# Decay attention into a three-way-max MLP: rows of decays on another DMA queue, head transposes in halves, the second batch's softmax sums on TensorE

## The chip, the cores and the metric

One core of a Trainium2 chip. The metric is the device time in microseconds of one execution. Engines: TensorE (PE, its weight loads PEld), VectorE (DVE), ScalarE (ACT), GpSimd (POOL) and SyncE (SP, which only issues DMAs here).

## The reference

Inputs: q, k, v of (8 batches, 8 heads, 576 positions, 64), decays f of (8, 8, 576), three weights of 512x768 and one of 768x512, all fp32 in effect.

```
scores = q k^T / 8 + cum[:, None] - cum[None, :]     # cum = cumsum(log(clip(f)))
scores = where(causal, -1e9, scores);  scores -= max(scores)
attn = exp(scores);  attn /= sum(attn) + 1e-9;  o = attn v
x = o as (4608 tokens, 512)
out = max(x w1, x w2, x w3) w_out                    # (4608, 512)
```

## The kernel before

Heads are numbered n = 0 to 63, eight to a batch; two heads are a pair. A head's scores are held transposed, keys on partitions and queries on columns, in two units: unit 2 has the first 256 queries (blocks of keys 0 and 1: 384 columns of scores), unit 1 the other 320 (1216 columns over five blocks of keys). For each unit: scores on TensorE into PSUM, a maximum over keys (DVE over the blocks, L695 to L706, then a POOL all-reduce over partitions, L716), the maximum subtracted by a further matmul pass, exp on ACT into probabilities (L734), and later the product with v (`values`).

**Batch 0** is treated apart. Its raw heads are loaded by SP (`load_raw`, L456) and transposed on TensorE by matmuls with an identity (`turn_head`, L463): for each of q and k three matmuls of 128 columns, whose result in PSUM holds even and odd positions of the head on the two halves of the partitions. Three of four copies to SBUF are ACT's (L481), one is DVE's (L479); each writes every second element of the head's row. Four PSUM banks serve two heads' turns. The cumulated decays are made in `decay` (L413): a scan on DVE, then row 64 of each head's keys is filled, for heads 0 and 1 by ACT itself and for heads 2 to 7 by six DMAs of 2304 bytes that ACT issues (L439). [...] Its sums of probabilities come from a column of ones beside v.

**Batches 1 to 7** use operands that are split in two fp32r parts; raw q and k are loaded four heads at a time (`load_quad`, L525), transposed and split by DVE and ACT, and rearranged into QS and KS by DMAs (`load_head`, L566). Their sums of probabilities are made outside TensorE (end of `scores`, L740 to L759): DVE adds the blocks of keys (L744 to L750; ACT copies 128 columns at L753), POOL adds over the partitions (L758) into Z, SP copies row 0 of Z into SC (`sums_row`, L862), and `finish_pair` (L867) adds 1e-9, takes the reciprocal, writes it to DRAM and reads it back spread over 64 partitions for each head, and multiplies the pair's output. The values of a pair (`values_pair`, L791) are fp32 matmuls of 64 weight columns each, one head in the lower and one in the upper half of the partitions of one PSUM bank (L802), five or two blocks of keys long.

**The MLP** of batch b (`moe`, L949) has 432 fp32r matmuls of 128x128 weights against 256 or 320 tokens (L906) and then the output matmuls of 512 columns (L935). It runs among the attention of batch b + 1. The weights (24 loads of 512 KB, L508) are split into two fp32r parts by ACT and DVE (L512 to L522) during batch 0.

**The order** is written by a planner (`Plan`, L49): each step is added with an engine, an estimated cost, the keys that it reads and writes and a priority; `emit` simulates the engines, takes from the ready steps of an engine the one with the lowest rank (priority less a share BLW of the work that hangs on it, L99) and so fixes each engine's program order. LAG, MORE and LATE are its delays between engines. A DMA step may not start before the eighth DMA before it is over (L137). [...]

Of the kernel before, what the change touches and what calls it, by code (L numbers as in the profile page):

```python
# [48 lines left out]
class Plan:  # L49
# [9 lines left out]

    ROOM = {"PE": (0.93, 0), "ACT": (1.0, -20.0), "DVE": (1.0, 0.0), "POOL": (1.0, 400.0), "SP": (1.0, 0)}  # L60
    LATE = 350.0
    MORE = (0.0, 100.0, 0.0, 0.0, 250.0)
    LIKE, HOLD = 4.0, 0.4

    def __init__(self):
# [21 lines left out]
    def emit(self):  # L87
# [8 lines left out]
        for i in reversed(range(n)):  # L96
            s = self.steps[i]
            down[i] = s[1] + s[5] + max((down[u] + 150 for u in users[i]), default=0.0)
        BLW = 0.21  # L99
        rank = [s[4] * 1.0 - BLW * down[i] / 12000 for i, s in enumerate(self.steps)]  # L100
        free, wait, live = {}, {}, {}
        for i, s in enumerate(self.steps):
# [8 lines left out]
        while done < n:  # L111
            best = None
            for e in free:
                t = free[e] if live[e] else (max(free[e], wait[e][0][0]) if wait[e] else None)
                if t is not None and (best is None or t < best[0]):
                    best = (t, e)
            t, e = best
            while wait[e] and wait[e][0][0] <= t:
                _, i = heapq.heappop(wait[e])
                heapq.heappush(live[e], (rank[i], i))  # L120

            here = live[e][0]
# [12 lines left out]
            if self.steps[i][5]:  # L135

                t = max(t, lanes[-8])  # L137
            begin[i] = t
            cost = (self.steps[i][1] - saved) * self.ROOM[e][0] + self.ROOM[e][1]
            end = t + cost  # L140
            if e == "PE":
                end = clock.run(t, cost, self.steps[i][6])
            free[e] = end
            done += 1
            if self.steps[i][5]:

                if self.steps[i][5] < 50 and e == "ACT":
                    end += 1850
                else:
                    end = moved = max(moved, end + 650) + self.steps[i][5]  # L150
                end += self.LATE
                lanes.append(end + 650)
            for u in users[i]:
                same = self.steps[u][0] == e
                lag = self.LAG["SP" if self.steps[i][5] else e][self.ENGINES.index(self.steps[u][0])]
                lag = 0 if same and e == "PE" else lag + self.MORE[self.ENGINES.index(self.steps[u][0])]
                ready[u] = max(ready[u], end + lag)
                left[u] -= 1
                if not left[u]:
                    heapq.heappush(wait[self.steps[u][0]], (ready[u], u))  # L160
# [24 lines left out]
def kernel(  # L185
# [18 lines left out]
    P = 128  # L204
# [44 lines left out]


    HEADS = [[sb(t, [P, 2 * S])] for t in ("qs0", "qs1", "ks0", "ks1")]
    for t in ("xh", "xl"):
        buf = sb(t, [P, 2, 2 * S])
        HEADS.append([buf[:, 0], buf[:, 1]])
    KQ = [x for group in HEADS for x in group]
    KF, QF = [x[:, 0:S] for x in KQ], [x[:, S:] for x in KQ]

# [28 lines left out]
    RAW = [sb(f"w{i}", [P, 1024], I32) for i in range(NW)]  # L286


    RAWQK = [x.bitcast(F32)[0:96, 0:768].rearrange("p (c x) -> p c x", c=2) for x in RAW[NW - H:]]
    spare = sb("hdl", [P, 512 + 2 * P], I32)  # L290
    XW = [sb("o", [P, 512], I32), spare[:, 0:512]]

# [120 lines left out]
    def decay():  # L413
# [18 lines left out]
        for n in range(2):  # L432
# [2 lines left out]
        c8 = UT[KT - 1][0:H, :]  # L435
        add("DVE", 540, lambda: nc.vector.tensor_scalar(c8, ft[0:H, :], -1.0 / scale, None, op0=ALU.mult),
            ["pf1"], [f"u{KT - 1}"], DP)
        for n in range(2, H):
            add("ACT", 600, lambda n=n: nc.scalar.dma_start(out=KF[n][64:65, :], in_=c8[n:n + 1, :]),  # L439
                [f"u{KT - 1}"], [f"kf{n}/2"], DP + n, 2304 / 360)  # L440
        add("DVE", 369, lambda: nc.vector.tensor_scalar(cs[:, 0, :], ft, -1.0, None, op0=ALU.mult),
            ["pf1"], ["cs"], DP)
        add("DVE", 669, lambda: nc.vector.scalar_tensor_tensor(
# [12 lines left out]
    def load_raw(n, prio):  # L456
        b, h = n // H, n % H
        for c, src in ((1, k), (0, q)):
            add("SP", 560, lambda c=c, src=src: nc.sync.dma_start(
                out=RAWQK[n][:, c], in_=src[b, h].rearrange("(p x) d -> p (x d)", p=96)),  # L460
                [], [f"raw{n}/{c}"], prio, 147456 / 330)

    def turn_head(n, prio):  # L463


        for c, buf, kc in ((0, QF, "qf"), (1, KF, "kf")):
            ps, kp = ((MPS[0], "mp0"), (MPS[1], "mp1"), (MPS[2], "mp2"), (TPS, "t0"))[2 * (n % 2) + c]

            def go(ps=ps, c=c):
                for a in range(3):  # L470
                    nc.tensor.matmul(ps[:, 96 * a:96 * a + 96], RAWQK[n][:, c, P * a:P * a + P],
                                     IDF[0:96, 0:96], start=a == 0, stop=True, skip_group_check=True)

            add("PE", 3 * 225, go, [f"raw{n}/{c}", "idf"], [kp], prio, rows=96)
            dst = buf[n][0:D, :].rearrange("d (p a e) -> d e a p", a=3, e=2)
            for e in range(2):
                src = ps[D * e:D * e + D, 0:288].rearrange("d (a p) -> d a p", a=3)
                if c == 0 and e == 0:
                    add("DVE", dve_cost(288), lambda dst=dst, src=src: nc.vector.tensor_copy(dst[:, 0], src), [kp], [f"{kc}{n}/0"], prio)  # L479
                else:  # L480
                    add("ACT", act_cost(288) + 115 * e, lambda dst=dst, src=src, e=e: nc.scalar.activation(  # L481
                        dst[:, e], src, AF.Copy), [kp], [f"{kc}{n}/{e}"], prio)


    def load_weights(step, prio):
# [131 lines left out]
    def scores(n, unit, prio):  # L617
# [111 lines left out]
        for bk, w, col in d["exps"]:  # L729
            if first:  # L730
                key = PFKEYS.get((unit, bk), [f"pf{name}"])
            else:
                key = [f"{pk}/{bk}"] if unit == 1 else [pk]
            add("ACT", act_cost(w), lambda bk=bk, w=w, col=col: nc.scalar.activation(  # L734
                px()[:, col:col + w], bank[bk][:, 0:w], AF.Exp, scale=sc), [kb[bk]], key, prio)
        if first:
            return


# [15 lines left out]
            add("DVE", dve_cost(P), add_blocks, [pk], ["s2/1"], prio + SP_)  # L755
        else:
            add("DVE", sum(dve_cost(w) for w in (320, 320, 192, 64)), add_blocks, [pk], ["s1"], prio + SP_)
        add("POOL", 450 + 2.6 * nq, lambda: nc.gpsimd.partition_all_reduce(  # L758
            Z[:, q0:q0 + nq], blocks_sum()[:, q0:q0 + nq], P, bass.bass_isa.ReduceOp.add), [f"s{unit}"], [f"z{unit}"], prio + SP_)  # L759

    def values(n, unit, prio):
# [29 lines left out]
    def values_pair(n, unit, prio):  # L791
# [74 lines left out]

    def finish_pair(pi, prio):  # L867
        i = pi % NU
        add("DVE", 130, lambda: nc.vector.tensor_scalar(SC, SC, 1e-9, None, op0=ALU.add), ["sc"], ["sc"], prio)
        add("DVE", 180, lambda: nc.vector.reciprocal(SC, SC), ["sc"], ["sc"], prio)  # L870
        row_dma(lambda: rdram[pi].rearrange("t (p c) -> (t p) c", p=32), lambda: SC, ["sc"], [f"rd{pi}"], prio)
        for j in range(2):
            row_dma(lambda j=j: R()[64 * j:64 * j + 64, :], lambda j=j: rdram[pi, j:j + 1, :].broadcast_to((64, S)),
                    [f"rd{pi}"], [f"r/{j}"], prio, 150000)
        add("DVE", dve_cost(S), lambda: nc.vector.tensor_tensor(U(i), U(i), R(), op=ALU.mult), [f"u{i}", "r"], [f"u{i}"], prio)

    def split_x(b, prio):
# [100 lines left out]
    QP = -0.2  # L978
    UO = 1
    LO = -2.55  # L980
    UP, VO, FO, XO = 0.4, 1.8, -0.95, -2.7
    HP, VP = -1.8, 0.35
    SP_ = 1.05
    HC, VO1, XO1, QP1, CB = -0.8, -1.0, -0.3, 0.4, -0.15
    order = (1, 2) if UO else (2, 1)
    for n in range(H):
        load_raw(n, n - 9.9)
    for n in range(H):
        turn_head(n, n - 5.1)
        if n % 2 == 0:  # L990
            load_v(n // 2, n - LEAD - VP)
    for unit, up in ((2, 0.0), (1, 0.5)):
# [27 lines left out]
    lag = 0.0  # L1020
# [63 lines left out]
```

## Time and profile before

| | |
|---|---|
| median of 3 runs | 915.48 us (915.07 to 915.65) |
| the profiled execution's own time | 919.88 us |
| its span, first to last instruction | 918.1 us |
| mean granted TensorE clock | 0.996 |
| PE busy | 896.9 us (98%), 6394 matmul records |
| PEld busy | 807.9 us (88%) |
| DVE busy | 678.9 us (74%) |
| ACT busy | 392.7 us (43%) |
| POOL busy | 455.4 us (50%) |
| queue of SP's DMAs | 94802 packets, 109.14 MB |
| queue of ACT's DMAs | 192 packets, 0.01 MB |

How to read it: the profile is of one execution, and the time of that execution lies 4.4 us above the median of the runs. Busy times of engines overlap; the end comes where one engine's work and its waits add up. Records of matmuls overlap one another (they are pipelined and their ends are modelled).

### The profile page before, as it was taken

The page shows a single profiled execution, that of the slowest core. Times are in us where ns is not written, and L with a number is a line of the kernel's source. Part 1 is how long each engine was busy: PE and PEld are TensorE (multiplying, and loading weights), DVE is VectorE, ACT ScalarE, POOL GpSimd, SP SyncE. Part 2 cuts the span into 40 slices and gives each one's busy share as a digit, 9 for nine tenths or more (in the row PEclk, how much of TensorE's full clock was granted, in tenths as well). Part 3 has the DMA queues.
Part 4 walks back from the last instruction along what each step waited for, and adds up shares of the span by engine and source line. Part 5 has one row for each costly group of instructions (what it writes and reads, how often), then busy time and mean ns, then how long its engine had stood idle before and what let it go on. Part 6 is the DMA issues. An engine that isn't in the chain of part 4 may idle for free.

```text
span 918.1 us, 17938 instructions
## 1 busy us (share of the span) xinstructions
PE 896.9 (98%) x6394; PEld 807.9 (88%) x6394; DVE 678.9 (74%) x1491; ACT 392.7 (43%) x900; POOL 455.4 (50%) x395
## 2 busy tenths in 40 slices
PE   6999999999999999999999999999999999999998
PEld 5899987888989898998989898998989898998998
DVE  5899998697958777796967777697877867662211
ACT  5897644444334433443334443344333434332111
POOL 4461456756455556546465464646556564641000
PEclk8999999999999999999999999999999999999999
DMA  7946245555435554634444454544464454401000
GB/s 219 304 130 165 65 125 135 154 119 133 131 98 141 129 144 113 157 91 127 127 117 130 121 156 105 135 118 106 118 143 148 105 152 117 116 14 37 1 35 24
DMA packets 95082, 110.29 MB, mean 120 GB/s; under 512 B 51617, under 2 KB 62625, under 8 KB 94994
## 3 DMA queue, kind: packets, MB, share of 16 engines
q1 hardware_dynamic: 94802, 109.14, 45.1%
q8 instruction: 51, 0.84, 0.4%
q14 instruction: 37, 0.30, 0.1%
q10 hardware_dynamic: 192, 0.01, 0.0%
HBM read 49.56 MB, written 9.86 MB: 65 GB/s over the span
## 4 chain that ended last, share of the span: by engine, by line
PE 74%; DVE 13%; DMA 5%; SPq 3%; issue 2%; ACT 2%; POOL 1%; ACTq 0%; DVEq 0%; POOLq 0%
PE mp L906 40%; PE mp L935 15%; PE s L646 10%; PE t L802 7%; DVE mx L706 2%; DVE va_s L750 2%; DMA w<-in_moe_w_dram 1%; DVE hl L535 1%; DVE tm L915 1%; SPq L368 1%; PE t L771 1%; DMA hl<-in_k_dram 1%; SPq L566 1%; DMA hl<-in_q_dram 1%; POOL z L758 1%
## 5 line engine op out<-in xcount | busy, mean ns | idle before, releaser
L906 PE MATMUL mp<-xh_r,w_r 128*128 128x320 f32 (+1 forms) x2160 | 461.6, 298 | 4.0 <-ACT tm L913 2.2
L906 PEld LDWEIGHTS mp<-xh_r,w_r 128*128 128x128 f32 x2160 | 355.6, 188 | 14.4 <-issue 5.4
L906 PE MATMUL mp<-xl_r,w_r 128*128 128x320 f32 (+1 forms) x1080 | 319.6, 296 | 0.0
L758 POOL PARTITION_ALL_REDUCE z<-va_s x112 | 226.2, 2019 | 183.1 <-DVE va_s L750 78.9
L716 POOL PARTITION_ALL_REDUCE gm<-mx x131 | 158.3, 1209 | 175.4 <-DVE mx L706 95.6
L906 PEld LDWEIGHTS mp<-xl_r,w_r 128*128 128x128 f32 x1080 | 203.3, 188 | 0.6
L915 DVE TENSOR_TENSOR tm<-mp,tm 128x256 f32<-128x256 f32 (+1 forms) x192 | 86.7, 452 | 68.3 <-PE mp L906 62.4
L646 PEld LDWEIGHTS s<-qs_r,ks_r 128*128 128x128 f32 (+1 forms) x784 | 115.1, 181 | 22.6 <-issue 14.5
L646 PE MATMUL s<-qs_r,ks_r 128*128 128x320 f32 (+4 forms) x784 | 131.4, 286 | 1.8 <-POOL qs_r L719 0.7
L935 PE MATMUL mp<-w_r,hmh_r 128*128 128x512 f32 (+1 forms) x396 | 123.3, 393 | 0.8 <-ACT w_r L521 0.6
L706 DVE TENSOR_TENSOR mx<-mx,s 128x320 f32<-128x320 f32 (+3 forms) x248 | 92.2, 372 | 21.5 <-PE s L646 12.1
L918 ACT ACTIVATE hmh_r<-tm 128x256 fp32r<-128x256 f32 x96 | 39.8, 414 | 127.6 <-DVE tm L915 127.1
L935 PEld LDWEIGHTS mp<-w_r,hmh_r 128*128 128x128 f32 x396 | 70.3, 188 | 16.5 <-issue 3.2
L935 PE MATMUL mp<-w_r,hml_r 128*128 128x512 f32 (+1 forms) x198 | 76.9, 388 | 0.0
L535 DVE STREAM_TRANSPOSE hl<-hl 128x576 f32<-128x576 f32 x56 | 68.6, 1243 | 3.7 <-DMA hl<-in_k_dram 3.6
L734 ACT ACTIVATE pf<-s 128x512 f32<-128x512 f32 (+4 forms) x107 | 49.1, 504 | 42.6 <-PE s L646 37.2
L913 ACT ACTIVATE tm<-mp 128x256 f32<-128x256 f32 (+1 forms) x96 | 39.4, 411 | 59.9 <-PE mp L906 55.5
L920 DVE TENSOR_TENSOR hml_r<-tm,hmh_r 128x256 fp32r<-128x256 f32 x96 | 48.9, 510 | 12.8 <-ACT hmh_r L918 12.6
L675 DVE TENSOR_TENSOR s<-s,mask 128x256 f32<-128x256 f32 x96 | 40.4, 421 | 21.3 <-PE s L646 21.2
L719 POOL CAST qs_r<-gm 1x256 fp32r<-1x256 f32 (+1 forms) x112 | 52.0, 464 | 7.2
L734 ACT ACTIVATE ph_f<-s 128x384 f32<-128x384 f32 x80 | 35.9, 505 | 39.9 <-PE s L646 34.8
L935 PEld LDWEIGHTS mp<-w_r,hml_r 128*128 128x128 f32 x198 | 37.2, 188 | 8.3
(207 smaller groups left out, 1281.0 us busy)
## 6 DMA issues: line engine op xcount, KB each, us to landing
qs_r<-hl SPq DMA_DIRECT2D x168, 144.0 KB, 2.6
ks_r<-hl SPq DMA_DIRECT2D x168, 144.0 KB, 2.7
w<-in_moe_w_dram SPq DMA_DIRECT2D x18, 512.0 KB, 6.3
out_dram<-o_r SPq DMA_DIRECT2D x35, 256.0 KB, 2.7
hl<-in_q_dram SPq DMA_DIRECT2D x14, 576.0 KB, 5.1
hl<-in_k_dram SPq DMA_DIRECT2D x14, 576.0 KB
r_r<-rdram SPq DMA_DIRECT2D x56, 144.0 KB, 3.0
vn<-in_v_dram SPq DMA_DIRECT2D x30, 128.0 KB, 5.1
```

The source lines that it names most:

```text
L535: add("DVE", 1085, lambda e=e, tt=tt, xs=xs: nc.vector.transpose(tt[:, e], xs[:, e]), [key + "0"], [key + "1"], prio)
L646: nc.tensor.matmul(bank[bk][0:l.shape[-1], col:col + w], l, rhs(qa, w), start=start and bk not in begun, stop=stop, skip_group_check=True)
L706: nc.vector.tensor_tensor(mt[:, a:a + w], mt[:, a:a + w], bank[bk][:, col:col + w], op=ALU.max)
L716: add("POOL", 450 + 2.6 * nq, lambda: nc.gpsimd.partition_all_reduce(gm, mt, P, bass.bass_isa.ReduceOp.max), [km, km + "a"], [kg], prio - CB)
L719: add("POOL", 130 + 0.9 * nq, lambda: nc.gpsimd.tensor_copy(QS(s)[96:97, 1, q0:q0 + nq], gm[96:97, :]), [kg], [kx], prio - CB)
L734: add("ACT", act_cost(w), lambda bk=bk, w=w, col=col: nc.scalar.activation(px()[:, col:col + w], bank[bk][:, 0:w], AF.Exp, scale=sc), [kb[ ...
L758: add("POOL", 450 + 2.6 * nq, lambda: nc.gpsimd.partition_all_reduce(Z[:, q0:q0 + nq], blocks_sum()[:, q0:q0 + nq], P, bass.bass_isa.Reduc ...
L802: nc.tensor.matmul(t[D * j:D * j + D, qa:qa + w], vn[:, j, c, 0:D], prs[j][0]()[:, col:col + w], start=x == 0, stop=True, skip_group_check ...
L906: nc.tensor.matmul(m, unit_w(i, fb)[:, w, kt, :], xx, start=kt == 0 and x == 0, stop=kt == KT - 1 and x == 2,)
L915: add("DVE", dve_cost(cn), lambda m=m: nc.vector.tensor_tensor(t, m, t, op=ALU.max), [km, kt_], [kt_], prio)
L920: add("DVE", dve_cost(w), lambda hh=hh, hl=hl, a=a, d=d, w=w: nc.vector.tensor_tensor(hl()[:, fb, d:d + w], t[:, a:a + w], hh()[:, fb, d:d ...
L935: nc.tensor.matmul(mp[:, 0:cn], l[:, fb, cs], unit_o(fb)[:, r, ds], start=fb == 0 and x == 0, stop=fb == FT - 1 and x == 2,)
```

## The change

- `decay`: the rows for heads 2 to 7 are issued by SP instead of ACT: one DMA each for heads 2 and 3, one for heads 4 and 5, one for heads 6 and 7 (their key buffers lie in one tile). They get a priority of their own.
- `load_raw` and `turn_head`: a raw head is loaded so that its first and second 288 positions lie side by side, 96 partitions with three positions of each half. Six matmuls of 64 columns of weights turn it, the first half's results on partitions 0 to 63 and the second's on 64 to 127; each writes 96 elements of a PSUM row with a step of 3. The copies then read and write plain rows.
- Batch 1 (n = 8 to 15): the adds on DVE and ACT and the all-reduce on POOL are left out. After the values of a pair and unit, matmuls with 32 columns of ones take the sums over keys into free columns of the same PSUM bank: heads in the two halves of the partitions, halves of the queries in two quarters of each, so four groups of 32 partitions. ACT copies them into ZR (two per pair), SP copies them into SC by two DMAs a pair in place of `sums_row`, and the reciprocals are written to DRAM by two DMAs instead of one.
- The planner's constants: BLW 0.21 to 0.19, DVE's further delay in MORE 0 to 125, LEAD, MLAG, WP, DP, QP, FO, XO, VP, SP_, XO1, QP1, `lag`, the turns' priority, the estimate of POOL's sum, and no special delay for ACT's short DMAs.

```
-    MORE = (0.0, 100.0, 0.0, 0.0, 250.0)
+    MORE = (0.0, 100.0, 125.0, 0.0, 250.0)
...
-        BLW = 0.21
+        BLW = 0.19
...
-                if self.steps[i][5] < 50 and e == "ACT":
-                    end += 1850
-                else:
-                    end = moved = max(moved, end + 650) + self.steps[i][5]
-                end += self.LATE
+                moved = max(moved, end + 650) + self.steps[i][5]
+                end = moved + self.LATE
...
+    def ZR():
+        return lazy("rx", [P, 384], F32)
...
-        for n in range(2, H):
-            add("ACT", 600, lambda n=n: nc.scalar.dma_start(out=KF[n][64:65, :], in_=c8[n:n + 1, :]),
-                [f"u{KT - 1}"], [f"kf{n}/2"], DP + n, 2304 / 360)
+        for n, e, dst in [(n, n + 1, KF[n][64:65, :]) for n in (2, 3)] + [
+                (4 + 2 * i, 6 + 2 * i, x[64:65, :, 0:S]) for i, x in enumerate(PAIRS)]:
+            add("SP", 560, lambda n=n, e=e, dst=dst: nc.sync.dma_start(out=dst, in_=c8[n:e, :]),
+                [f"u{KT - 1}"], [f"kf{x}/2" for x in range(n, e)], ROWS + n, 2304 / 360)
...
-                out=RAWQK[n][:, c], in_=src[b, h].rearrange("(p x) d -> p (x d)", p=96)),
+                out=RAWQK[n][:, c], in_=src[b, h].rearrange("(e p x) d -> p e (x d)", e=2, p=96)),
...
-                for a in range(3):
-                    nc.tensor.matmul(ps[:, 96 * a:96 * a + 96], RAWQK[n][:, c, P * a:P * a + P],
-                                     IDF[0:96, 0:96], start=a == 0, stop=True, skip_group_check=True)
+                for x in range(3):
+                    for e in range(2):
+                        nc.tensor.matmul(
+                            ps[D * e:D * e + D, 0:288].rearrange("d (p x) -> d x p", x=3)[:, x],
+                            RAWQK[n][:, c, e, D * x:D * x + D], IDF[0:96, 0:96], start=x == 0, stop=True, skip_group_check=True)
...
-                src = ps[D * e:D * e + D, 0:288].rearrange("d (a p) -> d a p", a=3)
+                dst, src = buf[n][0:D, 288 * e:288 * e + 288], ps[D * e:D * e + D, 0:288]
...
-        if first:
+        if n < 2 * H:
             return
...
-        add("POOL", 450 + 2.6 * nq, lambda: nc.gpsimd.partition_all_reduce(
+        add("POOL", 520 + 5.1 * nq, lambda: nc.gpsimd.partition_all_reduce(
...
+        wide = n < 2 * H
         add("PE", sum(4.04 * x[2] / 2.4 for x in cols) + 250, go, [k for _, k in prs] + [kv], [kt], prio, light=True)
+        if wide:
+            half, z0 = nq // 2, nq
+            runs = [[(max(qa, half * a), min(qa + w, half * a + half), col - qa) for c, qa, w, col in cols] for a in range(2)]
+            runs = [[x for x in xs if x[0] < x[1]] for xs in runs]
+            def total():
+                for x in range(max(map(len, runs))):
+                    for j in range(2):
+                        for a in range(2):
+                            if x < len(runs[a]):
+                                qa, qe, col = runs[a][x]
+                                r = 64 * j + 32 * a
+                                nc.tensor.matmul(
+                                    t[r:r + 32, z0 + qa - half * a:z0 + qe - half * a], ZR()[:, 288:320],
+                                    prs[j][0]()[:, col + qa:col + qe], start=False, stop=True, skip_group_check=True)
+            add("PE", max(sum(4.04 * (x[1] - x[0]) / 2.4 for x in xs) for xs in runs) + 100, total,
+                [k for _, k in prs] + ["ones", kt], [kt], prio)
+            add("ACT", act_cost(half), lambda: nc.scalar.activation(
+                ZR()[:, 128 * (2 - unit):128 * (2 - unit) + half], t[:, z0:z0 + half], AF.Copy), [kt], [f"zr{unit}"], prio)
...
+        wide = pi < 2 * NP
+        if wide:
+            for unit, nx, c0, z0 in ((2, 8, 0, 0), (1, 10, 8, 128)):
+                row_dma(lambda nx=nx, c0=c0: SC[:, c0:c0 + nx],
+                        lambda nx=nx, z0=z0: ZR()[:, z0:z0 + 16 * nx].rearrange("(r o) (y c) -> r o y c", r=4, c=nx)[:, 0],
+                        [f"zr{unit}"], [f"sc/{unit - 1}"], prio)
...
-    LEAD, MLAG, WP, WR = 1.95, -0.2, -0.6, 0.55
-    DP = -9.9
+    LEAD, MLAG, WP, WR = 2.1, -0.1, 0.7, 0.55
+    DP = -10.9
+    ROWS = -4.0
...
-    UP, VO, FO, XO = 0.4, 1.8, -0.95, -2.7
-    HP, VP = -1.8, 0.35
-    SP_ = 1.05
-    HC, VO1, XO1, QP1, CB = -0.8, -1.0, -0.3, 0.4, -0.15
+    UP, VO, FO, XO = 0.4, 1.8, 0.25, -3.1
+    HP, VP = -1.8, 0.6
+    SP_ = 1.25
+    HC, VO1, XO1, QP1, CB = -0.8, -1.0, -2.3, 0.7, -0.15
...
-        turn_head(n, n - 5.1)
+        turn_head(n, n - 5.6)
...
-        sums_row(n, p + FO)
+        if n >= 2 * H:
+            sums_row(n, p + FO)
```

## Rows read from the trace of the kernel before

**Rows 1.** The page, busy time of each engine over the span.

```profile
PE 896.9 (98%) x6394; PEld 807.9 (88%) x6394; DVE 678.9 (74%) x1491; ACT 392.7 (43%) x900; POOL 455.4 (50%) x395
```

**Rows 2.** Busy time by stretch: width, engines' busy us (instructions), granted clock, DMA share, GB/s.

```profile
10.00:25.00 15.00, 11.44 (x59) 9.53 (x59) 4.87 (x11) 7.70 (x13) 1.69 (x2) 0.77 0.81 226
25.00:80.00 55.00, 52.40 (x422) 49.38 (x422) 51.94 (x107) 50.46 (x107) 26.67 (x26) 1.00 0.66 197
80.00:110.00 30.00, 30.00 (x262) 29.95 (x261) 29.13 (x58) 19.98 (x49) 9.02 (x9) 1.00 0.48 136
110.00:185.00 75.00, 69.97 (x508) 59.91 (x507) 64.86 (x141) 32.34 (x78) 48.18 (x38) 1.00 0.51 130
215.00:836.00 621.00, 617.91 (x4385) 553.31 (x4384) 474.70 (x1064) 246.62 (x578) 344.44 (x281) 1.00 0.47 120
```

Its five busy columns are PE, PEld, DVE, ACT and POOL.

**Rows 3.** Chain of waits, first 20 us: start, us, what.

```profile
9.35 7.50 DMA w<-in_moe_w_dram
16.87 0.51 ACTq L439
```

**Rows 4.** Timeline, 9 to 19 us: start, us, engine, line, what [idle before, releaser].

```profile
9.39 0.91 PE L471 MATMUL mp<-hdl,w 96*128 96x96 f32 x6 [1.90 <-DVE qs L479]
...
10.57 1.58 ACTq L439 DMA_DIRECT2D ks<-u  x2
...
11.50 2.32 SPq L368 DMA_DIRECT2D vn<-in_v_dram  x3
...
13.05 1.35 ACT L481 ACTIVATE qs<-mp 64x288 f32<-64x288 f32 x2 [3.02 <-issue]
...
14.46 0.91 PE L471 MATMUL mp<-hdl,w 96*128 96x96 f32 x6 [1.56 <-ACT qs L481]
...
17.43 0.67 ACT L481 ACTIVATE qs<-mp 64x288 f32<-64x288 f32 x1 [3.02 <-DMA w<-in_moe_w_dram]
...
18.23 0.92 SPq L508 DMA_DIRECT2D w<-in_moe_w_dram  x2
```

**Rows 5.** Timeline, 25 us: the first split of a weight.

```profile
25.62 0.41 DVE L514 TENSOR_SCALAR o<-w 128x512 int32<-128x512 int32 x1
```

**Rows 6.** Groups by line and shape: count, busy us, mean ns, idle before.

```profile
L471 PE MATMUL mp<-hdl,w 96*128 96x96 f32 x72 | 11.3, 306 | 5.5 <-ACT qs L481 3.6 <-DVE qs L479 1.9
...
L783 ACT ACTIVATE u<-mp 64x256 f32<-64x256 f32 x8 | 3.0, 371 | 0.1
...
L481 ACT ACTIVATE xl<-mp 64x288 f32<-64x288 f32 x4 | 2.6, 703 | 0.6 <-PE mp L471 0.5
```

**Rows 7.** Chain of waits, fp32 matmuls: batch 0's values, batch 1's pair.

```profile
104.32 1.21 PE t L771 x10
...
148.95 2.21 PE t L802 x20
...
152.67 0.80 PE t L802 x8
```

**Rows 8.** Timeline of PE, 148 us: from MLP matmuls to those of values.

```profile
148.49 0.31 PE L906 MATMUL mp<-xl_r,w_r 128*128 128x320 f32 x1
148.64 0.31 PE L906 MATMUL mp<-xh_r,w_r 128*128 128x320 f32 x1
148.88 0.27 PE L802 MATMUL t<-pf,vl 128*64 128x64 f32 x1
```

**Rows 9.** The adds' tile from 110 to 215 us: width, DVE, ACT, POOL, clock, DMA, GB/s.

```profile
110.00:215.00 105.00, 19.56 (x45) 3.09 (x10) 36.48 (x18) 1.00 0.50 127
```

**Rows 10.** Chain of waits, 137 to 182 us.

```profile
137.16 2.33 POOL z L758
...
174.38 3.96 DMA ks_r<-hl
...
178.42 3.52 DMA hl<-in_k_dram
```

More of the change, by code (lines that the diff above doesn't have):

```diff
@@ L251 @@
     HEADS = [[sb(t, [P, 2 * S])] for t in ("qs0", "qs1", "ks0", "ks1")]
-    for t in ("xh", "xl"):
-        buf = sb(t, [P, 2, 2 * S])
-        HEADS.append([buf[:, 0], buf[:, 1]])
+    PAIRS = [sb(t, [P, 2, 2 * S]) for t in ("xh", "xl")]
+    HEADS += [[x[:, 0], x[:, 1]] for x in PAIRS]
     KQ = [x for group in HEADS for x in group]
@@ L286 @@
     RAW = [sb(f"w{i}", [P, 1024], I32) for i in range(NW)]
-    RAWQK = [x.bitcast(F32)[0:96, 0:768].rearrange("p (c x) -> p c x", c=2) for x in RAW[NW - H:]]
+    RAWQK = [x.bitcast(F32)[0:96, 0:768].rearrange("p (c e x) -> p c e x", c=2, e=2) for x in RAW[NW - H:]]
     spare = sb("hdl", [P, 512 + 2 * P], I32)
@@ L469, in go @@
             def go(ps=ps, c=c):
-                for a in range(3):
-                    nc.tensor.matmul(ps[:, 96 * a:96 * a + 96], RAWQK[n][:, c, P * a:P * a + P],
-                                     IDF[0:96, 0:96], start=a == 0, stop=True, skip_group_check=True)
-            add("PE", 3 * 225, go, [f"raw{n}/{c}", "idf"], [kp], prio, rows=96)
-            dst = buf[n][0:D, :].rearrange("d (p a e) -> d e a p", a=3, e=2)
+                for x in range(3):
[3 more added lines that the diff above has]
+                            RAWQK[n][:, c, e, D * x:D * x + D], IDF[0:96, 0:96], start=x == 0, stop=True, skip_group_check=True)
+            add("PE", 700, go, [f"raw{n}/{c}", "idf"], [kp], prio, rows=96)
             for e in range(2):
-                src = ps[D * e:D * e + D, 0:288].rearrange("d (a p) -> d a p", a=3)
+                dst, src = buf[n][0:D, 288 * e:288 * e + 288], ps[D * e:D * e + D, 0:288]
                 if c == 0 and e == 0:
-                    add("DVE", dve_cost(288), lambda dst=dst, src=src: nc.vector.tensor_copy(dst[:, 0], src), [kp], [f"{kc}{n}/0"], prio)
+                    add("DVE", dve_cost(288), lambda dst=dst, src=src: nc.vector.tensor_copy(dst, src), [kp], [f"{kc}{n}/0"], prio)
                 else:
-                    add("ACT", act_cost(288) + 115 * e, lambda dst=dst, src=src, e=e: nc.scalar.activation(
-                        dst[:, e], src, AF.Copy), [kp], [f"{kc}{n}/{e}"], prio)
+                    add("ACT", act_cost(288) + 115 * e, lambda dst=dst, src=src: nc.scalar.activation(
+                        dst, src, AF.Copy), [kp], [f"{kc}{n}/{e}"], prio)
     def load_weights(step, prio):
@@ L868, in finish_pair @@
         i = pi % NU
+        wide = pi < 2 * NP
[4 more added lines that the diff above has]
+                        [f"zr{unit}"], [f"sc/{unit - 1}"], prio)
         add("DVE", 130, lambda: nc.vector.tensor_scalar(SC, SC, 1e-9, None, op0=ALU.add), ["sc"], ["sc"], prio)
         add("DVE", 180, lambda: nc.vector.reciprocal(SC, SC), ["sc"], ["sc"], prio)
-        row_dma(lambda: rdram[pi].rearrange("t (p c) -> (t p) c", p=32), lambda: SC, ["sc"], [f"rd{pi}"], prio)
+        if wide:
+            for unit, nx, c0 in ((2, 8, 0), (1, 10, 8)):
+                row_dma(lambda nx=nx, unit=unit: rdram[pi][:, Q0[unit]:Q0[unit] + NQ[unit]].rearrange("t (y c) -> t y c", c=nx),
+                        lambda nx=nx, c0=c0: SC[:, c0:c0 + nx], ["sc"], [f"rd{pi}/{unit}"], prio)
+        else:
+            row_dma(lambda: rdram[pi].rearrange("t (p c) -> (t p) c", p=32), lambda: SC, ["sc"], [f"rd{pi}/1"], prio)
         for j in range(2):
             row_dma(lambda j=j: R()[64 * j:64 * j + 64, :], lambda j=j: rdram[pi, j:j + 1, :].broadcast_to((64, S)),
-                    [f"rd{pi}"], [f"r/{j}"], prio, 150000)
+                    [f"rd{pi}/1", f"rd{pi}/2"], [f"r/{j}"], prio, 150000)
         add("DVE", dve_cost(S), lambda: nc.vector.tensor_tensor(U(i), U(i), R(), op=ALU.mult), [f"u{i}", "r"], [f"u{i}"], prio)
@@ L970, in moe @@
                 done += 18 * mm_cost(512, P)
-    LEAD, MLAG, WP, WR = 1.95, -0.2, -0.6, 0.55
-    DP = -9.9
+    LEAD, MLAG, WP, WR = 2.1, -0.1, 0.7, 0.55
+    DP = -10.9
     DPW = 4.0
+    ROWS = -4.0
     warm_up()
     decay()
-    QP = -0.2
+    QP = -0.3
     UO = 1
     LO = -2.55
-    UP, VO, FO, XO = 0.4, 1.8, -0.95, -2.7
-    HP, VP = -1.8, 0.35
-    SP_ = 1.05
-    HC, VO1, XO1, QP1, CB = -0.8, -1.0, -0.3, 0.4, -0.15
+    UP, VO, FO, XO = 0.4, 1.8, 0.25, -3.1
+    HP, VP = -1.8, 0.6
+    SP_ = 1.25
+    HC, VO1, XO1, QP1, CB = -0.8, -1.0, -2.3, 0.7, -0.15
     order = (1, 2) if UO else (2, 1)
@@ L988 @@
     for n in range(H):
-        turn_head(n, n - 5.1)
+        turn_head(n, n - 5.6)
         if n % 2 == 0:
             load_v(n // 2, n - LEAD - VP)
-    for unit, up in ((2, 0.0), (1, 0.5)):
+    for unit, up in ((2, 0.0), (1, 0.7)):
         for n in range(H):
@@ L1019 @@
         retire([c + t for c in ("mx", "pf")] + [f"mx{t}a"], [f"{t}{x}" for x in fbs])
-    lag = 0.0
+    lag = 0.15
     moe(0, lambda x: H + lag + H * x)
@@ L1028 @@
     retire(["vn3"], ["s1", "s2"])
+    retire(["rx"], ["zr1", "zr2", "ones"])
+    add("POOL", 150, lambda: nc.gpsimd.memset(ZR()[:, 288:320], 1.0), w=["ones"], prio=p)
     for i in range(2):
```

## The prediction

> **What bounds the kernel now.** I read the engines' busy times first: PE is busy for 896.9 of 918.1 us, everything else far less [rows 1]. So the end is set by how much matmul time there is plus the time in which PE waits or runs slowly, and the second question is where those waits lie. The table of stretches answers it [rows 2]. From 80 to 110 us PE is busy for 30.00 of 30 us, and from 215 to 836 us it idles for 3.1 us in all: there, matmul time alone counts. PE loses time in three places. [...] From 25 to 80 us it idles 2.60 us, while DVE is busy for 51.94 and ACT for 50.46 of 55. From 110 to 185 us it idles 5.03 us with DVE busy for 64.86 of 75. Idle time of PE is too low a measure here, since a matmul's record is longer than its slot; the weight loads show it better. PEld is busy for 89% of 215 to 836 us but 80% of 110 to 185 us; at 89% the same loads would need 59.91/0.891 = 67.2 us, 7.8 us less.
>
> Then the chain of waits, for the first place [rows 3]: a weight load lands 7.50 us after 9.35 us, and what it releases is not a consumer of weights but an issue on ACT's queue, a row of decays. The timeline shows the consequence [rows 4]. ACT issues the rows at 10.57 and later, and its own copies of turned heads start only at 13.05 and 17.43, after 3.02 us of idle each. PE, which turns four operands (two heads) and then needs a bank freed by those copies, does one further turn at 9.39 and otherwise warm-up matmuls until 14.46. DVE starts its first weight split at 25.62 [rows 5], though it is free for 10 of the 15 us from 10 to 25 [rows 2].
>
> **The change, part by part.**
>
> *Rows of decays on SP (start).* Six issues leave ACT, four come to SP (two of them carry two heads). ACT gets back its two idle spells, 6.0 us, and the copies that free PE's banks can follow one another from about 10 us. SP pays four issues at some 0.8 us, as for the six on ACT or the three of v at 11.50 [rows 4], 3.1 us. SP stands without an issue from 13.82 to 18.23 anyway, so I put this at nothing; without that cover v and the weights behind the rows would come 3.1 us later. What is late next: the raw heads, whose last issue precedes the weights at 9.35, and then the weights themselves, at 16.85; DVE can start splits there instead of at 25.62. Bounds for the gain: 0 (the rows stand in SP's queue until the same weight load lands) and 3.56 + 3.45 = 7.0 us (all that PE loses there). [...]
>
> *Turning in halves.* A turn was 3 matmuls of 128 columns of weights, 6 records in 0.91 us [rows 4]; it becomes 6 matmuls of 64 columns, 12 records, on two halves of the array. The trace has pairs of halves side by side elsewhere (below), so I count no change on PE. What changes surely is the evacuation: ACT's copies wrote every second element and took 703 ns for 64x288; copies of 64x256 into a plain row take 371 ns, so some 400 ns for 288 [rows 6]. 24 copies x 0.3 = 7.2 us come off ACT in the first 40 us, and 8 DVE copies give perhaps 0.2 us each. From 25 to 80 us both are nearly full, so part of PE's 2.60 us should come back: bounds 0 and 2.6, taken 1.6. The raw loads come in runs half as long (768 instead of 1536 bytes); no row shows that size, and I leave it at 0.
>
> On PE the halves write every third element of a PSUM row, which no row of before does. The nearest are L471's own records, 306 ns a record for 96 columns [rows 6]: a turn could cost what it does now, or twice that, 16 x 0.91 = 14.6 us more in all (a rival, below). [...]
>
> *Sums of batch 1 on PE, cost.* For each of the four pairs: the unit of 320 queries has 64+160x4 = 704 columns in its longer half and 512 in the other, the unit of 256 has 256 and 128, each for two heads. Four column groups (two heads x two halves) can run at once. What a column costs: serial fp32, 704 columns in 1.21 us = 1.72 ns; two heads at once, 1216 columns each in 2.21 us = 1.82 ns, and 384 in 0.80 us [rows 7]. So two groups overlap almost wholly. Four groups: (704+256) x 1.82 = 1.75 us, and a change of tiling, seen where L802 follows L906 in 0.24 us instead of 0.15 [rows 8], twice: 1.95 us a pair, 7.8 us for four. Lower bound 960 x 1.72 x 4 + 0.4 = 7.0. Upper bound, nothing overlaps: 3200 columns x 1.72 = 5.5 us a pair, 22 us. I take 7.8, by the row that shows two groups at once. All of it is on the path, since PE is what bounds.
>
> [...]
>
> *The same, what leaves.* The 16 reductions at 36.48/18 = 2.03 us leave POOL (32 us) and 40 adds at 19.56/45 = 0.43 us leave DVE (17 us) [rows 9]. POOL is off the path save for single pieces (2.33 us at 137 us in the chain [rows 10]). DVE is on it from 110 to 145 us. On the other hand, PE's waits after 155 us end in transfers too: 3.96 us for keys and 3.52 us for a raw quad at 174 to 182 us [rows 10], which the edit does not touch. Bounds for 110 to 185 us: 0 and the 7.8 us above; I take 6.0, since DVE loses more work there than PE waits. SP's reads of the sums stay at two a pair and the writes of reciprocals become two, four more issues in 100 us: nothing, hidden under matmuls of other steps. ACT gets two copies a pair of some 0.3 us and loses as many adds' copies: nothing. The values' bank is held longer by the sums and a copy, about 2 us a pair; PE has MoE matmuls to do then, so nothing.
>
> *Plan constants.* They reorder every queue. From 215 to 836 us the waits to be won are 3.1 us, and as much could be added; I take -0.2.
>
> Sum: -5.0 - 1.6 - 6.0 - 0.2 + 7.8 = -5.0 us. The profiled execution took 919.88 us (1.8 outside its span), 4.4 above the median of 915.48; its 5.0 us are taken off the median: 910.5. With the likeliest case's own spread, 907 to 914.
>
> **Rivals.**
> 1. *The start gains nothing.* The rows wait in SP's queue for the same weight load, and heads 2 to 7 come no earlier. For: the release shown in rows 3 is a landing, not ACT's own slowness. Against: ACT's copies no longer stand behind it. 910.5 + 5.0 = 915.5.
> 2. *The batch 1 stretch stays as it is*, since its waits pass to the transfers of rows 10. Only about 1 of the 6.0 us comes back: 915.5.
> 3. *Slower: the four groups do not overlap.* Place: the new matmuls between about 145 and 215 us; price 22.0 instead of 7.8, so 924.7. It decides as soon as the sums exceed 12.8 us, which is about 1.7 groups at once. Against it stands the overlap of two in rows 7.
> 4. *Slower: the strided PSUM writes double a turn.* 14.6 us more PE work in the first 40 us, against 8.2 us of loss there that the change would otherwise use (3.56 + 3.45 and about half of 2.60): the start gains 5.0 and 1.6 less and PE is 1 to 2 us later than now, so about 918.5. It decides from some 0.4 us a turn.
> 5. *Everything comes back*: start 7.0, 25 to 80 us 2.6, 110 to 185 us 7.8, about 904.
>
> **Chances.** Forecast 0.52, rival 1 0.14, rival 2 0.12, rival 3 0.07, rival 4 0.05, rival 5 0.10. A measurement of this kernel can tell about 0.2% (1.8 us) from no change. Faster by more: nearly all of the forecast (0.49), rival 5, and a fifth of rivals 1 and 2, together 0.64; slower: rivals 3 and 4 and 0.08 of rivals 1 and 2, 0.20; the rest 0.16. The range runs from rival 5 to just short of rival 4: 904.5 to 918.
>
> **What would show it.** Start: no ACT issues of rows; copies of turned heads from about 10 us without 3 us spells; the first weight split before 20 us; a granted clock near 1 from 10 to 25 us. Turns: copies near 0.40 us, 12 records in at most 0.9 us. Sums: four records starting within some 20 ns, about 1.3 us for the unit of 320 and 0.5 us for that of 256. Batch 1: PE idle below 1.5 us from 110 to 185 us and PEld near 89%. From 215 us on: stages of the same length. The prediction is wrong if the start gains under 2 us, if the sums cost over 12 us, or if the steady stretch moves by more than 3 us.

## The result and the profile after

The median went from 915.31 us (915.07 to 915.65, 4 runs) to 908.27 us (907.59 to 908.40, 4 runs): 7.0 us less. The ratio of runs is 0.9896, 95% interval 0.9849 to 0.9943 (the ratio of the medians, 0.9923, lies in it). The forecast was 910.5, its range 904.5 to 918.

The profiled executions differ by more, 919.88 against 907.59 us, 12.3 us. Each part of that is set against the medians below.

The page, busy time of each engine, beside [rows 1]:

```profile
PE 894.0 (99%) x6682; PEld 808.5 (89%) x6682; DVE 643.5 (71%) x1451; ACT 387.5 (43%) x900; POOL 426.8 (47%) x380
```

PE has 7.6 us more work in the sums (below) and is yet busy for 2.9 us less. DVE lost 35.4 us of busy time and POOL 28.6. The stretches, with the columns of [rows 2]:

```profile
10.00:25.00 15.00, 14.66 (x191) 12.80 (x189) 8.29 (x22) 11.16 (x28) 5.51 (x6) 1.00 0.81 220
25.00:80.00 55.00, 52.00 (x426) 49.14 (x423) 53.20 (x108) 43.77 (x99) 24.24 (x25) 1.00 0.82 248
80.00:110.00 30.00, 30.00 (x261) 30.00 (x260) 29.02 (x62) 20.59 (x49) 9.44 (x9) 1.00 0.16 48
110.00:185.00 75.00, 74.73 (x648) 65.25 (x647) 50.93 (x103) 33.35 (x78) 24.02 (x27) 1.00 0.52 134
215.00:823.40 608.40, 606.89 (x4325) 546.41 (x4324) 454.44 (x1049) 244.50 (x570) 339.24 (x276) 1.00 0.47 121
```

From 10 to 25 us PE idles 0.34 us instead of 3.56 and the clock is 1.00 instead of 0.77. From 110 to 185 us it idles 0.27 us instead of 5.03, and PEld is busy for 87% instead of 80%. From 25 to 80 us nothing came back: 3.00 us of idle time against 2.60.

The start, as in [rows 4]:

```profile
8.92 0.72 PE L471 MATMUL mp<-hdl,w 96*64 96x96 f32 x12 [1.50 <-DVE qs L479]
9.86 1.25 ACT L481 ACTIVATE qs<-mp 64x288 f32<-64x288 f32 x3
10.73 1.21 PE L471 MATMUL mp<-hdl,w 96*64 96x96 f32 x24 [0.34 <-ACT qs L481]
11.96 2.22 SPq L438 DMA_DIRECT2D ks<-u  x2
14.22 0.67 SPq L438 DMA_DIRECT2D xh<-u  x1
14.94 0.58 SPq L438 DMA_DIRECT2D xl<-u  x1
20.52 0.42 DVE L514 TENSOR_SCALAR o<-w 128x512 int32<-128x512 int32 x1
```

The rows now stand in SP's queue (L438), ACT copies from 9.86 us on, two turns take 1.21 us, and the first split of a weight on DVE begins at 20.52 instead of 25.62 [rows 5]. Before, two whole turns in a row took 1.52 us at a clock of 1.00:

```profile
25.04 1.52 PE L471 MATMUL mp<-hdl,w 96*128 96x96 f32 x12
```

The groups of turns and copies in the first 45 us of after, beside [rows 6]:

```profile
L471 PE MATMUL mp<-hdl,w 96*64 96x96 f32 x144 | 7.7, 255 | 1.8 <-DVE qs L479 1.5 <-ACT qs L481 0.3
...
L481 ACT ACTIVATE xl<-mp 64x288 f32<-64x288 f32 x4 | 1.5, 404 | 0.3 <-DVE xl L479 0.3
```

The sums in the chain of waits (start, us, what), one of four pairs beside [rows 7], and the timeline at their start:

```profile
147.94 1.34 PE t L821 x32
...
151.97 0.57 PE t L821 x12
```

```profile
147.87 0.25 PE L821 MATMUL t<-pf,rx_r 128*32 128x32 f32 x2
147.88 0.25 PE L821 MATMUL t<-ph_f,rx_r 128*32 128x32 f32 x2
```

Four groups start within 20 ns, and a pair takes 1.34 + 0.57 = 1.91 us, four pairs 7.64.

**Where the 12.3 us lie.** I follow four points of the trace: the last matmul of the first layers of batch 0's MLP (432 of 128x128), the last values of batch 1, the same MLP point for batch 1, and for batch 7.

```
us                      MLP 0   values 1   MLP 1   MLP 0 to 1   MLP 7
before                  202.2      200.8   308.5        106.3   906.0
after                   194.5      190.5   300.0        105.5   893.5
```

To MLP 0: -7.7. From there to MLP 1: -0.8. MLP 1 to MLP 7: 597.5 before and 593.5 after, -4.0; behind that +0.2. The -8.5 up to MLP 1 stands against 7.0 between the medians. Of the 71 executions of before beside the experiments, 62 took 914.1 to 917.0 us and nine 918.5 to 923.6, so the profiled one is among the longer ones. The -4.0 of the steady stretch is probably not the change's: the profiled execution of before is 4.6 us above its median, and in the profiles of the twelve experiments below, two of them with the old constants throughout, this stretch takes 593 to 596 us. No second profile of before was taken, so this stays open.

The -7.7 up to MLP 0 by parts: PE's idle time falls from 14.7 to 6.8 us (two windows of the trace that end there), -8.0; the lower clock goes, 15 x 0.23 by [rows 2], -3.4; the turns take 0.72 instead of 0.91 us alone and 1.21 instead of 1.52 us for two in a row, 16 x 0.15 to 0.19 = -2.4 to -3.0 (an estimate); the sums add 7.6. That makes -6.2 to -6.8; the rest, about 1 us, is not placed.

### The profile page after: what moved, and what is told of

Read it like the earlier page. It is cut to its first block, busy times and chain, and to the rows that moved or that the text cites. A ratio compares the mean times of both kernels' runs of the same rounds, so it can differ in the third digit from the quotient of the medians.

```text
span 905.5 us, 18417 instructions
## 1 busy us (share of the span) xinstructions
PE 894.0 (99%) x6682; PEld 808.5 (89%) x6682; DVE 643.5 (71%) x1451; ACT 387.5 (43%) x900; POOL 426.8 (47%) x380
## 3 DMA queue, kind: packets, MB, share of 16 engines
HBM read 49.56 MB, written 9.86 MB: 66 GB/s over the span
## 4 chain that ended last, share of the span: by engine, by line
PE 94%; DVE 2%; ACT 2%; DMA 1%; issue 1%; SPq 0%; ACTq 0%; DVEq 0%
PE mp L939 50%; PE mp L968 17%; PE s L646 13%; PE t L802 9%; PE t L771 2%; PE t L821 1%; DMA w<-in_moe_w_dram 1%; PE mp L771 1%; PE s L662 0%; ACT hl L539 0%; PE t L857 0%; SPq L438 0%; ACT ph_f L734 0%; PE mp L646 0%; DVE va_s L750 0%
## 5 line engine op out<-in xcount | busy, mean ns | idle before, releaser
L758 POOL PARTITION_ALL_REDUCE z<-va_s x96 | 193.1, 2012 | 162.3 <-DVE va_s L750 61.2
L719 POOL CAST qs_r<-gm 1x256 fp32r<-1x256 f32 (+1 forms) x112 | 56.8, 508 | 7.1
L713 ACT ACTIVATE mx<-s 128x320 f32<-128x320 f32 x56 | 24.4, 436 | 51.8 <-DVE s L680 44.1
```

What stands on the lines that cost most here:

```text
L719: add("POOL", 130 + 0.9 * nq, lambda: nc.gpsimd.tensor_copy(QS(s)[96:97, 1, q0:q0 + nq], gm[96:97, :]), [kg], [kx], prio - CB)
L758: add("POOL", 520 + 5.1 * nq, lambda: nc.gpsimd.partition_all_reduce(Z[:, q0:q0 + nq], blocks_sum()[:, q0:q0 + nq], P, bass.bass_isa.Reduc ...
```

## Experiments

In some, the planner makes its order anew from the changed steps ("replanned"); in others the order of after is kept, so that only the edit differs. Ratios are to before, with 95% intervals. Where a time is set against after, the medians are compared. They come from different sessions, between which the median of before went from 915.31 to 916.19, so such a difference holds to about 1 us.

**1. Rows on ACT again, replanned.**

```
-            add("SP", 560, lambda n=n, e=e, dst=dst: nc.sync.dma_start(out=dst, in_=c8[n:e, :]),
+            add("ACT", 600, lambda n=n: nc.scalar.dma_start(out=KF[n][64:65, :], in_=c8[n:n + 1, :]),
```

> The changed kernel with the six rows of decays issued by ACT again (and the planner's old special delay for them). Theory A, the terms of the prediction: the start loses its 5.0 us, so about 913.3 us against 908.3 of the changed kernel; ACT idle for two spells of 3 us between 10 and 18 us, PE idle 2 us or more from 10 to 25 us. Rival R, the order that the constants write is what gains: within 1.5 us of 908.3, with ACT's spells covered by other work.

917.59 us (914.33 to 921.05), ratio 1.0016 [0.9998, 1.0034]: 9 us above after. The timeline of its start:

```profile
12.38 4.43 ACTq L441 DMA_DIRECT2D xh<-u  x2
...
16.86 0.82 ACT L484 ACTIVATE qs<-mp 64x288 f32<-64x288 f32 x2 [7.04 <-DMA ks<-u]
17.74 1.09 PE L474 MATMUL mp<-hdl,w 96*64 96x96 f32 x12 [5.20 <-ACT qs L484]
```

The edit also brings back the planner's old delay for ACT's short DMAs, and there are six issues again. While issues wait in its queue ACT idles for 7.04 us, and PE waits 5.20 us for the copy behind them. Theory A's mechanism is shown; the higher price is that of the rows and of the new order together.

**2. The four issues by ACT, same order.**

```
-            ... nc.sync.dma_start(out=dst, in_=c8[n:e, :])
+            ... nc.scalar.dma_start(out=dst, in_=c8[n:e, :])
```

> The changed kernel, every engine's order as it is, but the four issues of rows stand in ACT's queue instead of SP's, at the same place of the plan. Theory A (ACT's queue stands while an issue waits, and the start loses what PE waits for it): two or more us slower, up to the 9 us that the re-planned kernel with rows on ACT lost. Rival R (the loss there came from the order that the plan took with rows on ACT, not from the queue): within 1 us of 908.3.

910.07 us (907.97 to 911.76), 0.9914 [0.9880, 0.9948]: 1.8 us above after by the medians, but the ranges and the intervals overlap, so a price is not shown. Timeline:

```profile
12.59 0.63 ACTq L438 DMA_DIRECT2D ks<-u  x1
14.30 1.13 ACTq L438 DMA_DIRECT2D xh<-u  x1
15.47 0.41 ACT L481 ACTIVATE xh<-mp 64x288 f32<-64x288 f32 x1 [1.36 <-PE mp L471]
```

No issue stands long here (1.13 us at most). So by the medians the engine alone costs some 2 us at most. Experiment 1 has six issues for four and another place for them among the copies; no run parts these two.

**3 and 4. Whole turns again: replanned, and in the same order.**

```
-                        nc.tensor.matmul(ps[D * e:D * e + D, 0:288].rearrange("d (p x) -> d x p", x=3)[:, x],
-                            RAWQK[n][:, c, e, D * x:D * x + D], ...)
+                    nc.tensor.matmul(ps[:, 96 * a:96 * a + 96], RAWQK[n][:, c, P * a:P * a + P], ...)
```

> The changed kernel with the old loads and turns of raw heads (128 columns of weights, copies that write every second element). Theory A: 1.6 us slower, 909.9. Theory A with the shorter turns of the trace after (12 records in 0.72 us or less against 6 in 0.91): up to 16 x 0.25 = 4 us slower, 912.3. Rival R: within 1 us of 908.3. Copies near 0.70 us again in all cases.

> The changed kernel with the old loads, turns and strided copies, the plan's costs and so every engine's order as they are. Theory A: 16 turns longer by 0.2 to 0.25 us and copies longer by 0.3 us on ACT, so 2 to 4 us slower, 910 to 912. Rival R, the 11 us that the re-planned kernel with whole turns lost came from another order: within 1.5 us of 908.3. Rival T, turns are worth all of it: 917 or more here too.

Replanned 919.69 us (918.95 to 921.38), 1.0033 [1.0014, 1.0052], farther than any theory had it; in the same order 917.10 us (915.44 to 918.10), 0.9999 [0.9979, 1.0019]. So the turns, with their loads and copies, are worth about 9 us and not 1.6, as rival T had it. The stretch from 10 to 25 us of the second, and its turns:

```profile
10.00:25.00 15.00, 14.48 (x81) 13.62 (x80) 6.70 (x14) 11.14 (x19) 1.85 (x2) 0.66 0.73 200
```

```profile
9.41 0.91 PE L470 MATMUL mp<-hdl,w 96*128 96x96 f32 x6 [1.84 <-DVE qs L478]
...
13.92 1.49 PE L470 MATMUL t<-hdl,w 96*128 96x96 f32 x6
...
16.75 2.82 PE L470 MATMUL mp<-hdl,w 96*128 96x96 f32 x12
```

PE is as busy as in after (14.48 against 14.66 us), but at a mean clock of 0.66: 15 x 0.34 = 5.1 us. The clock is 1.00 up to 10 us, 0.68 from 10 to 15 and 0.50 from 15 to 20. Before it fell, PE had waited 1.84 us up to the turn at 9.41 and 0.52 us up to one at 11.49; in after it waited 1.50 and 0.34 us at the same places, and the clock stayed. After the fall a turn takes 1.49 us (at 13.92) instead of 0.91 (at 9.41), and two in a row take 2.82 us where the clock is 0.50 (at 16.75), against 1.52 in before at 1.00.

**5. Whole turns with plain copies, same order**, to part the turns on PE from ACT's copies. Batch 0's positions then stand in another order. The edit against experiment 4:

```
-            dst = buf[n][0:D, :].rearrange("d (p a e) -> d e a p", a=3, e=2)
+                dst, src = buf[n][0:D, 288 * e:288 * e + 288], ps[D * e:D * e + D, 0:288]
```

> The changed kernel in the same order with whole turns (128 columns of weights, old loads), but copies that write plain rows, so batch 0's positions stand in another order. It parts the 9 us that whole turns with strided copies lost. Theory C, the copies' 0.3 us each is the price (they pace the banks that PE needs): 909 to 910. Theory P, the slower turns on TensorE are the price: 914 or more. Halves of each: 911 to 913.

914.09 us, 0.9963 [0.9938, 0.9988], in two groups: four runs at 907.8 to 910.1, eight at 912.8 to 916.3. The profiled one took 916.1 us; its turns on the timeline:

```profile
14.88 1.49 PE L470 MATMUL t<-hdl,w 96*128 96x96 f32 x6
...
24.32 0.83 PE L470 MATMUL t<-hdl,w 96*128 96x96 f32 x6
```

The median is theory P's, and 3.0 us below experiment 4, which is what the copies are worth. But the first four runs show that whole turns can cost under 2 us, while the others lose 4.5 to 8 us. In the profiled one the turns take 1.49 us each until 24 us. That is the pace of the turns of experiment 4 after its clock had fallen (0.50 from 15 to 20 us), though this trace holds no record of the clock before 24.3 us. The mean clock that is on record for each run fits: 0.998 to 1.000 for the four, 0.993 to 0.994 for the three from 912.8 to 914.2 us (0.0065 x 914 = 6 us). The five from 915.1 us on have 0.999 to 1.000, as the profiled one has, whose record begins late. I read it that most of the price of whole turns is the lower clock. It is not shown, since no run changes the clock alone, and what makes one run fall into it and another not is open.

**6. Halved turns that write plain PSUM rows, same order.** Batch 0's positions again stand in another order.

```
-   ps[D * e:D * e + D, 0:288].rearrange("d (p x) -> d x p", x=3)[:, x]
+   ps[D * e:D * e + D, 96 * x:96 * x + 96]
```

> The changed kernel in the same order with halved turns that write plain stretches of 96 elements of a PSUM row instead of every third element (batch 0's positions stand in another order). Theory A, the step of 3 costs TensorE nothing for fp32: turns as long as with it (12 records in some 0.7 us) and 908.3 within 1 us. [...]

908.07 us (907.84 to 908.86), 0.9910 [0.9882, 0.9939]. The timeline has the same durations as after:

```profile
8.92 0.72 PE L471 MATMUL mp<-hdl,w 96*64 96x96 f32 x12 [0.97 <-DVE qs L479]
10.74 1.21 PE L471 MATMUL mp<-hdl,w 96*64 96x96 f32 x24 [0.34 <-ACT qs L481]
```

A step of three in PSUM costs these fp32 matmuls nothing: one turn takes 0.72 us and two take 1.21 us with it (after) and without it. Rival 4 is out.

**7. Only the last block's sums, same order.** The sums over the other blocks of keys are left out.

```
-                            if x < len(runs[a]):
+                            if x == len(runs[a]) - 1:
```

> The changed kernel in the same order, with sums over the last block of keys alone (the other blocks of batch 1's sums are left out): 1.3 us in place of 1.91 us of matmuls less some 1.15 us a pair, 4.6 us less TensorE work in all. Theory A (PE bounds there, all of the price is on the path): 4 to 4.6 us faster, about 904. Rival H (the sums fill time in which PE would wait): within 1 us of 908.3.

904.11 us (903.35 to 906.12), 0.9851 [0.9815, 0.9887]: 4.2 us below after, where theory A had 4.6. What the sums cost on PE is on the path. Its profile shows one thing more. The start has the edit and the order of after, and yet:

```profile
10.00:25.00 15.00, 15.00 (x177) 12.82 (x176) 9.06 (x24) 11.57 (x28) 5.29 (x6) 0.91 0.83 229
```

So halved turns do not always keep the clock at 1.00, and the 1.00 of the profile of after is that of one execution.

**8 and 9. Fewer or no sums on PE, replanned**: for two of the four pairs, and for none.

```
-        if n < 2 * H:
+        if n < 12:       # experiment 8; "n < 8" in experiment 9; so too in values_pair, finish_pair, sums_row
```

> The changed kernel with sums on TensorE for the first two pairs of batch 1 alone (planned anew). Theory A: half of the 7.6 us price saved and most of DVE's relief kept, 904.5 to 906. Rival R, a plan made anew under constants that were set for another set of steps loses more than the step is worth: 912 or more.

> The changed kernel with batch 1's sums on DVE and POOL again. Theory A: the sums cost 7.6 us on TensorE and give back 6.0, so without them 1.6 us faster, 906.7, with PE idle some 5 us more from 110 to 185 us. Rival D, the relief of DVE is worth more than the matmuls cost: 2 us or more slower, 910.3 or above, with PE idle 9 us or more there. Rival N, that relief brings nothing: 7 us faster, 901.

913.16 us (912.03 to 915.72), 0.9970 [0.9953, 0.9986], and 924.94 us (923.64 to 926.05), 1.0092 [1.0072, 1.0113]. The sums cost PE 7.6 us, and without them the kernel is 16.7 us slower. By these numbers what leaves DVE and POOL is worth far more, under these constants, than the 6 us that I had put on it, and half of it is not enough. But both kernels are planned anew, and 912 or more is also what rival R of experiment 8 had for a new order under constants set for other steps: no run parts the relief from the order. The windows at the turn of the stages, experiment 9 and then after:

```profile
110.00:185.00 75.00, 70.98 (x500) 61.28 (x499) 59.22 (x125) 30.98 (x73) 43.33 (x34) 0.98 0.48 124
185.00:215.00 30.00, 24.55 (x151) 19.92 (x150) 22.82 (x46) 12.17 (x25) 19.36 (x15) 0.97 0.50 129
215.00:240.00 25.00, 23.80 (x147) 21.42 (x147) 18.72 (x48) 10.71 (x26) 14.56 (x12) 0.83 0.51 127
```

```profile
185.00:215.00 30.00, 30.00 (x232) 25.64 (x233) 21.61 (x54) 13.50 (x33) 15.84 (x13) 1.00 0.63 159
215.00:240.00 25.00, 25.00 (x177) 24.54 (x176) 21.78 (x47) 10.07 (x24) 12.20 (x12) 1.00 0.47 128
```

The loss is less before 185 us (4.0 us of idle time, not the 9 of rival D) than after it: from 185 to 240 us PE idles 6.7 us, and the clock takes 0.9 + 4.3 us more.

**10. The sums alone, in before.** The diff's parts for the sums, old constants.

> The kernel before with batch 1's sums on TensorE alone (old constants, rows on ACT, whole turns). Theory A: 7.8 - 6.0 = 1.8 us slower than before, 917.2. Rival D, DVE's relief is worth more than the matmuls cost whatever the constants: 2 us or more faster, 913 or less. Rival R, each part needs the constants that go with it: 5 us or more slower, 920 or more.

920.19 us (919.29 to 926.37), 1.0039 [1.0015, 1.0063]: 3.6 us slower by the ratio, between theory A and rival R. Its windows, and the second of before:

```profile
110.00:185.00 75.00, 74.22 (x654) 65.00 (x653) 50.80 (x107) 32.72 (x80) 22.66 (x28) 1.00 0.52 134
...
215.00:240.00 25.00, 22.30 (x144) 20.21 (x143) 21.77 (x41) 10.40 (x24) 12.99 (x10) 0.86 0.46 125
```

```profile
215.00:240.00 25.00, 25.00 (x182) 23.32 (x181) 19.88 (x46) 9.92 (x25) 14.56 (x13) 1.00 0.52 143
```

From 110 to 185 us PE idles 0.78 instead of 5.03 us, just as forecast, and from 215 to 240 us it loses 2.7 us to idle time and 3.5 us to the clock, and before loses nothing.

**11. Rows on SP and halved turns, in before.** The diff's parts in `decay`, `load_raw` and `turn_head` and, with the rows, the end of the planner's special delay for ACT's short DMAs; otherwise old constants.

> The kernel before with rows on SP and halved turns, old constants, sums on DVE and POOL. Theory A: the start gains 5 to 9 us whatever the constants, 906 to 910. Rival R: within 2 us of before (915.3) or slower, with what the start wins lost again by 200 us.

916.80 us (914.92 to 919.76), 1.0006 [0.9989, 1.0024]. In the profile MLP 0 ends 13.7 us earlier than in before, and by the medians nothing of it is left at the end, as rival R had it. PE idles where the stages meet:

```profile
185.00:215.00 30.00, 25.26 (x146) 20.89 (x145) 22.56 (x43) 11.95 (x24) 14.97 (x12) 0.94 0.46 117
```

**12. The new constants alone, in before.**

> The kernel before with the planner's new constants alone (rows on ACT, whole turns, sums on DVE and POOL). Theory A: -0.2 us, 915.1 against 915.3 of before. Rival R, the order does most of it: 3 to 5 us faster, 910 to 912.

922.21 us (919.72 to 926.03), 1.0063 [1.0040, 1.0087]: 6 us slower, where I had -0.2. No run has all three edits under the old constants, so what the new ones are worth beside them is not shown.

**What they say together.** The first three points in the profiles of all of them:

```
us                                MLP 0   values 1   MLP 1   MLP 0 to 1
before                            202.2      200.8   308.5        106.3
after                             194.5      190.5   300.0        105.5
1  rows on ACT, replanned         202.5      196.6   307.8        105.3
2  issues by ACT, same order      194.4      190.5   299.8        105.4
4  whole turns, same order        202.0      198.0   307.4        105.4
5  whole turns, plain copies      201.5      197.6   307.5        105.9
6  plain PSUM rows                195.3      190.9   300.6        105.3
7  short sums                     192.6      188.1   298.1        105.5
12 constants alone                211.2      207.9   317.4        106.2
3  whole turns, replanned         199.7      200.4   314.0        114.3
8  sums of two pairs              190.9      196.4   304.9        114.0
11 rows and turns in before       188.5      196.2   306.4        117.9
10 sums alone in before           194.3      201.2   312.5        118.2
9  no sums on PE                  187.8      204.5   314.5        126.7
```

Where batch 1's last values come before the end of batch 0's MLP, the next MLP needs 105 to 106 us; where they come later, it needs 114 to 127 us. In the first case there are MLP matmuls left for PE while attention waits for other engines. In the second they are used up, PE waits, and the clock falls besides (experiment 9: 0.83). So the time looks like that of the later of two strands. Sums alone or a faster start alone bring MLP 0 forward by 8 to 14 us and batch 1's attention not at all or by less, and the gain is given back. The whole change brings both forward, by 7.7 and 10.3 us. I take this from the order of two points in fourteen traces; no run moved one of them and nothing else. The second point alone does nearly as well: MLP 1 follows batch 1's last values after 107.7 to 111.2 us in the first case and 108.5 to 113.6 us in the second. What speaks for two strands is that in the first case the distance from MLP 0 varies by 1 us only.

## Why the prediction was right

The sign and the size were right, -5.0 forecast and -7.0 measured, by a sum of which only one large term was well sized.

- **Sums on PE, +7.8:** measured 7.64 (4 x 1.91), and on the path by experiment 7. Two groups' overlap did carry over to four; rival 3 is out.
- **Start, -5.0:** the mechanism held point by point: ACT's 3 us spells went, the clock of the profile is 1.00, rival 1 is out. The 5.0 was my estimate between the bounds of 0 and 7.0, and no run shows it as a term of its own. What the profiles show is the idle time and the lower clock that went, 3.2 + 3.45 = 6.7 us (3.45 is 15 x 0.23 by [rows 2]), but not for the rows alone: with the rows on SP and whole turns the clock is still 0.50 from 15 to 20 us (experiment 4). One sign just failed: the first split came at 20.52, not before 20. What the rows' queue is worth by itself is some 2 us at most in the same order, and 9 where the planner puts six of them among the copies.
- **Turns, -1.6:** the worst sized, 9 us by experiment 4. The step that failed is "I count no change on PE". A turn fell from 0.91 to 0.72 us, two in a row from 1.52 to 1.21, and in the trace of experiment 4 the clock is 0.66 with PE idle for 0.52 of 15 us, a loss for which this term had nothing. The copies came out as forecast (404 ns for "some 400"), yet PE's idle time from 25 to 80 us, where I booked the gain, did not fall.
- **Relief of DVE and POOL, -6.0:** PE's idle time from 110 to 185 us fell by 4.8 us and PEld went to 87%, near the forecast (the adds on DVE, L743 to L750, fell from 130 to 105 us over the run, 26 us where I had 17). Its worth is another matter: alone in before, with the sums' price, it makes +3.6 (experiment 10); within after, taking it back costs 16.7 us net of the 7.6 that PE saves, new order included (experiment 9). By the table above, the kernel without it lies on the other side, and I had treated it as a length of waits.
- **Constants, -0.2:** +6 alone in before. They do not fit the old kernel; that they fit the other parts is argued, not shown. With the parts' own results (+0.6, +3.6 and +5.8 us by ratios 1.0006, 1.0039 and 1.0063) a sum would be +10, where the whole is -7.0: adding terms was itself the weak point of the method. Two terms too small on the gain's side and a coupling that I had not seen came out near the forecast partly by luck.
- **Steady stretch:** -4.0 us between the profiles, past the 3 us that I had set as a sign of error. It is probably the profiled execution of before; open, as said.

Rival 2 is out by the stretch from 110 to 185 us. Rival 5, everything back, came nearer than its chance said: idle time there and the start's clock did come back almost wholly, and only 25 to 80 us gave nothing. Its time was added up wrongly: 910.5 - 2.0 - 1.0 - 1.8 is 905.7, not about 904, so the range's lower end of 904.5 lies 1.2 us below what its own terms give.

No version that leaves no work out was measurably faster than after.

## What to carry to other kernels

Where one stage's matmuls fill the waits of the next stage's attention, find the two points at which each runs out. In these traces a gain on one strand paid only until the other ended last, so price edits together and not one by one. Before counting an edit on the bounding engine as nothing, look at what its groups of records take at either clock level (two whole turns 1.52 us at 1.00 and 2.82 us at 0.50 here), and at the clock beside the busy time. Constants of a planner that win with one set of steps can lose with another (6 us here), and undoing one edit under a replanned order measures the order too; keep the order if the edit is what you want to know.

## What was not expected of the hardware

- From 10 to 25 us PE is busy for 14.48 us at a mean clock of 0.66 with whole fp32 turns (experiment 4), for 14.66 us at 1.00 with halves on two column groups (after) and for 15.00 us at 0.91 with the same halves (experiment 7). Busy time doesn't tell the clock.
- At a clock of 1.00 two turns as 64-column halves take 1.21 us, and as 128-column matmuls 1.52 us (before, at 25.04 us).
- Four groups of 32 columns, 704 columns in the longest, take 1.34 us; 704 columns in series took 1.21 [rows 7].
- A step of three elements in PSUM costs these fp32 matmuls nothing (0.72 and 1.21 us with and without it).
